# More planned reserve behind transposing DMAs, and loads one group further ahead, in a fused attention and MLP kernel

## Chip, cores, metric

The kernel runs on one core of a Trainium2 chip. The metric is the device time of one execution in microseconds (us). An engine is named as in the profile: PE is TensorE, PEld its weight loads, DVE VectorE, ACT ScalarE, POOL GpSimd, SP SyncE. SP computes nothing here; it issues transposing DMAs. POOL issues nearly all loads, ACT the stores.

## What is computed

Sliding-window attention over 8 batches of 8 heads, 576 positions of 64 channels, followed by a two-layer MLP on the 4608 resulting rows.

```python
scores = q @ k.T / sqrt(64)                      # per batch and head
scores = where(abs(i - j) <= 32, scores, -1e9)
attn = softmax(scores) @ v
x = attn.transpose(0, 2, 1, 3).reshape(4608, 512)
h = maximum(x @ w_in, 0.0)                       # w_in: 512 x 2048
out = (h * h) @ w_out                            # w_out: 2048 x 512
```

Inputs and output are float32; the kernel works in bf16 with float32 sums.

## The kernel before, in words

**Tiles.** Attention is cut into 24 groups G = 3b + g, of 192 query rows each (three per batch b). A group's two windows of keys give its scores by 16 small matmuls (L547); ACT takes the exponential (L571), DVE multiplies with the band mask (L576), PE multiplies with v (L604), DVE normalises into `xa` and `xb` (L626). The MLP works on tokens: the first layer (`mm1`, L719) in blocks of 192, 256 or, from token 2048 on, 512 tokens, each cut into pieces of up to 16 matmuls that share one PSUM bank; ACT takes the relu (L725), DVE squares it into `gt` (L728). The second layer (`mm2`, L739) works on blocks u of 128 tokens, each in four segments of four 128x512 matmuls. "Block 13.0" is segment 0 of u = 13.

**How data come to their places.** For each group POOL issues two loads of k and two of q (L376, `load_qk`) and two of v (L425, `load_v`); they cast to bf16. q and k must be transposed before the scores. For the first two batches (groups 0 to 5) PE does this (`turn_pe`). From group 6 on SP does it by transposing DMAs (L506, `turn_dma`), two for k and two for q. The attention result is transposed as well, into `xt`: by PE for groups 0 to 2, by two SP DMAs from group 3 on, one from `xa` (64 rows, L699) and one from `xb` (128 rows, L702). A first-layer block needs the `xt` of all its tokens.

**Who sets the order.** The program records every operation with an engine, what it reads and writes, a planned duration and a key, and then plans the whole run with a list scheduler (`schedule`): whenever an engine is free in the plan, it takes the ready operation with the lowest key. The result is a fixed order on each engine. On the chip each engine works through its list and waits on semaphores where an input isn't there yet; planned times themselves are not enforced. So a constant of the plan changes nothing but the order.

**Keys.** One unit is 64 tokens. A group's scores have key 3G - 13 (`LEAD`), its SP transposes 3G - 16, its `xt` transposes 3G - 12.8 and 3G - 12.5; a piece of the first layer has its token number / 64 (plus a share for its place in the block), a segment of the second layer 2u + 9 + seg / 2.

**What the plan assumes of a DMA.** It is issued for `dur` ns (for a transposing DMA `TISS` = 1340), queued, served as so many packets of so many ns (`move`), and its data count as landed after a further `LANDQ` (2000 ns) plus a `slack` of its own:

```python
dma=(f"t{t}{G % 6}", G), key=key, dur=TISS, move=(h // 4, TMOVE), name=f"td{t}{b}{g}", slack=TSLACK)   # L508
it[3].end = now + LANDQ + it[3].slack                                                                  # L163
```

`TSLACK` belongs to the q and k transposes (h // 4 is 20 to 28 packets), `XSLACK` to the two `xt` transposes (16 and 32 packets), and `TMOVE`, ns per packet, to both. Loads have `LSLACK` (5000).

**What releases a load.** A load's key sets its place in the recording, and it also gets a real dependency: `after=self.moe`, the last scores or first-layer piece recorded before it (L378, L428). With the key 3G - 13 - 9 (`AHEAD`) of a group from 6 on, this is the scores of group G - 3. On the chip POOL, which takes its list in order, waits there on a semaphore of PE. Raw q and k have six buffers, as does v, so a group's load may overwrite what group G - 6 has used.

Of the kernel before, what the change touches and what calls it, by code (L numbers as in the profile page):

```python
# [22 lines left out]
LEAD = 13.0  # L23
LAG = 9.0
AHEAD = 9.0
TISS = 1340
TMOVE = 25
NVR = 24
VKEY = 10.0
TSLACK = 1000  # L30
XSLACK = 1000
LSLACK = 5000
NCLR = 1
LANDQ = 2000
# [232 lines left out]
class Gen:  # L267
# [233 lines left out]
    def turn_dma(self, t, b, g, key):  # L501
# [3 lines left out]
        for x in range(2):  # L505
            self.p.rec("SP", lambda e, x=x: e.dma_start(dst[:, :, h * x:h * x + h], raw[0:h, x, :], transpose=True),  # L506
                       reads=[("raw", t, G % NRAW, x)], writes=[(t + "t", b % 2, g) if x else (t + "h", b % 2, g)],
                       dma=(f"t{t}{G % 6}", G), key=key, dur=TISS, move=(h // 4, TMOVE), name=f"td{t}{b}{g}", slack=TSLACK)  # L508

# [124 lines left out]
    def xturn(self, G):  # L634
# [4 lines left out]
        if G < NXT:  # L639
# [48 lines left out]
            if two:  # L688
                for x, (c0, c1) in enumerate(((0, 64), (64, 192))):
# [9 lines left out]
        self.p.rec("SP", lambda e: e.dma_start(self.XT[:, :, r:r + 64], xa[64:128, :], transpose=True),  # L699
                   reads=[("xa", G % 3)], writes=wr[:1], dma=(f"xa{G % 3}", G), key=key - 0.3, dur=TISS, move=(16, TMOVE), name=f"T{G}a",  # L700
                   slack=XSLACK)
        self.p.rec("SP", lambda e: e.dma_start(self.XT[:, :, r + 64:r + 192], xb[:], transpose=True),  # L702
                   reads=[("xb", G % 3)], writes=wr[1:], dma=(f"xb{G % 3}", G), key=key, dur=TISS, move=(32, TMOVE), name=f"T{G}b", slack=XSLACK)

# [76 lines left out]
    def build(self):  # L781
        p = self.p
        self.k1 = 0
        self.moe = None
        K = -100.0
        self.setup_idle()
        self.setup_iota(K + IOTA)
        self.setup_id(K)
        self.setup_mask(2, K + 1)
        self.setup_bias(2, K + 1.1)  # L790
        self.setup_mask(1, K + 2)
        self.setup_bias(1, K + 2.1)
        self.setup_k(0, K + 0.5)
        self.setup_v(0, K + 1.5)
        self.setup_v(1, VSET[0])
        self.setup_v(2, VSET[1])
        self.setup_mask(0, MKEY[0])
        self.setup_mask(3, MKEY[1])
        for i in range(3, NV):
            self.setup_v(i, -9)  # L800
        self.setup_k(1, -9)
        for n, it in enumerate(self.opening()):
            kd, a = it[0], it[1:]
            key = K + n
            if kd == "w1":
                self.load_w1(a[0], key)
            elif kd == "w2":
                self.load_w2(a[0], key)
            elif kd == "v":
                self.load_v(*divmod(a[0], 3), key, a[1:])  # L810
            elif kd[0] == "h":
                self.load_hw(kd[1], a[0], key)
            else:
                self.load_pair(kd, *divmod(a[0], 3), key)
        for g in (1, 2, 4, 5):
            self.copy_v(g, K + 7 if g < 3 else 3 * g - LEAD - AHEAD)
        todo = []

        def at(key, f, *a):
            todo.append((key, len(todo), f, a))  # L820

        for G in range(NG):
            b, g = divmod(G, 3)
            if b > 1:
                key = 3 * G - LEAD - AHEAD
                for t in "kq":
                    at(key, self.load_pair if G < NPAIR else self.load_qk, t, b, g, key)
                at(key, self.load_v, b, g, key)
                if g and G < NVR:
                    key = 3 * G - LEAD - 0.5 if G >= VCS else key  # L830
                    at(key + 0.01, self.copy_v, G, key - VKEY if G >= VCS else key)
            for t in "kq":
                key = 3 * G - LEAD - (0.6 if b < NTURN else 3)
                at(key, self.turn_pe if b < NTURN else self.turn_dma, t, b, g, key)
            for ws in ((0,), (1,)) if G < NSPLIT else ((0, 1),):
                at(3 * G - LEAD + 0.3 * ws[0], self.scores, G, ws)
            for w in range(2):
                at(3 * G - LEAD + 0.3 * w + 0.1, self.pv, G, w)
            at(3 * G - LEAD + 0.5, self.xturn, G)
        t0 = 0  # L840
        while t0 < NTOK:
            n = FIRST[t0] if t0 in FIRST else 192 if t0 < 768 else 256 if t0 < T512 else 512
            m = min(512 // n, 4)
            for d in range(0, 16, m):
                key = t0 / 64 + d / 16 * n / 64
                at(key, self.mm1, t0, n, list(range(d, d + m)), key)
            t0 += n
        at(500, self.mm2_last, NBLK - 1, 500)
        for u in range(NBLK - 1):
            for seg in range(4):  # L850
                at(2 * u + LAG + seg * 0.5, self.mm2, u, seg, 2 * u + LAG + seg * 0.5)
        for key, _, f, a in sorted(todo, key=lambda x: x[:2]):
            f(*a)
        p.schedule()
        with self.nc.Block():
            dsems, dcount = p.emit()
            for s in dsems:
                if s[0] == "o":
                    self.nc.sync.wait_ge(dsems[s], dcount[s])
# [35 lines left out]
```

## Time and profile before

| | |
|---|---|
| median of 3 runs | 302.69 us (302.65 to 303.72) |
| the profiled execution: own time | 303.58 us |
| its span, first to last instruction | 301.5 us |
| granted PE clock | 1.000 |
| first layer, L719 | 144.6 us in 896 matmuls |
| second layer, L739 | 139.2 us in 560 matmuls |
| SP transposes of q and k, L506 | 72, 1.25 us each to issue (median), landing 2.3 / 5.6 / 8.2 us after issue (least, median, most) |
| POOL waiting for scores before a load | 78.6 us in 15 waits |

Busy times of one engine add up to more than the span, because matmuls overlap in the array: the start-to-start distance of two matmuls says more than the duration of one. A line of the timeline gives start, duration, engine, line, operation, out<-in, the count of instructions merged into it, and in brackets the idle time before it with the releaser that the profile infers. The releaser is the one that came last by the semaphore records; where that engine's result is no input, it was another, often a DMA. In a table by stretches each engine has its busy time and in brackets its instructions; then come the granted clock, the share of the DMA engines (over 1 where packets overlap) and GB/s.

The 16 DMA engines are busy in 27 of the page's 40 slices, up to some 210 us, when the last loads and most transposes are done; after that mostly output is written. POOL has nothing more to do from 198 us on.

### The profile page before, as it was taken

What the parts mean: (1) busy time and instruction counts of PE and PEld (TensorE: products, weight loads), DVE (VectorE), ACT (ScalarE), POOL (GpSimd) and SP (SyncE); (2) the same over time, 40 slices, a digit from 0 to 9 for tenths busy, and PEclk for the clock granted to TensorE, in tenths of its full rate; (3) what the DMA queues carried; (4) which work ended last, traced back from release to release, by engine and by line L of the source; (5) the groups of instructions that cost most, each with busy time, mean ns of one, the idle gap of its engine ahead of it and who ended that gap; (6) DMA issues with size and microseconds to landing.
All of it is one profiled execution on the core that took longest, in us unless ns stands there. A gap on an engine that the chain in (4) does not pass through costs nothing.

```text
span 301.5 us, 6250 instructions
## 1 busy us (share of the span) xinstructions
PE 294.1 (98%) x2431; PEld 171.2 (57%) x2431; DVE 166.7 (55%) x385; ACT 161.5 (54%) x250; POOL 107.2 (36%) x143
## 2 busy tenths in 40 slices
PE   7899999999999999999989999999999999999997
PEld 3488876757667777664444545444445444444445
DVE  6898786736677776655756656456456322222100
ACT  4487845746456676644656645646636344443312
POOL 8992326526546654454664526320000000000000
PEclk9999999999999999999999999999999999999999
DMA  9999999999999999999999999994111200100112
GB/s 171 176 205 184 195 178 164 160 221 154 189 155 187 154 151 160 163 154 195 127 176 185 176 151 138 185 126 105 55 37 55 67 35 35 37 35 36 37 70 104
DMA packets 160636, 39.83 MB, mean 132 GB/s; under 512 B 149984, under 2 KB 156128, under 8 KB 160608
## 3 DMA queue, kind: packets, MB, share of 16 engines
q0 software_dynamic: 106016, 17.93, 82.8%
q1 hardware_dynamic: 49264, 12.14, 29.0%
q10 hardware_dynamic: 5328, 9.37, 9.4%
q8 instruction: 19, 0.31, 0.4%
q14 instruction: 9, 0.07, 0.1%
HBM read 36.70 MB, written 9.44 MB: 153 GB/s over the span
## 4 chain that ended last, share of the span: by engine, by line
PE 90%; DMA 5%; POOL 3%; DVE 1%; ACT 0%; issue 0%; POOLq 0%; ACTq 0%
PE ht L719 40%; PE outp L739 40%; DMA w<-in_moe_w_in_dram 5%; PE at L547 4%; PE at L604 4%; POOL v L425 1%; POOL w L438 1%; PE at L467 1%; PE ht L764 1%; PE outp L764 1%; POOL kpair L408 1%; POOL qpair L408 1%; ACT rt L725 0%; DVE gt L728 0%; DVE xa L626 0%
## 5 line engine op out<-in xcount | busy, mean ns | idle before, releaser
L719 PE MATMUL ht<-xt,w 128*128 128x256 bf16 (+2 forms) x896 | 144.6, 303 | 0.2 <-DMA w<-in_moe_w_in_dram 0.2
L739 PE MATMUL outp<-w,gt 128*128 128x512 bf16 x560 | 139.2, 379 | 0.0
L725 ACT ACTIVATE rt<-ht 128x512 bf16<-128x512 f32 (+1 forms) x152 | 86.3, 577 | 87.8 <-PE ht L719 83.9
L719 PEld LDWEIGHTS ht<-xt,w 128*128 128x128 bf16 x896 | 81.0, 98 | 43.6 <-DMA w<-in_moe_w_in_dram 0.3
L728 DVE TENSOR_TENSOR gt<-rt 128x512 bf16<-128x512 bf16 (+1 forms) x152 | 61.6, 408 | 61.2 <-ACT rt L725 59.2
L739 PEld LDWEIGHTS outp<-w,gt 128*128 128x128 bf16 x560 | 52.3, 98 | 55.3 <-ACT oe L749 0.8
L376 POOL DMA_DIRECT2D kraw<-in_k_dram x36 | 27.8, 780 | 89.9 <-PE at L547 78.6
L571 ACT ACTIVATE e<-at 128x1024 bf16<-128x1024 f32 x46 | 44.8, 1021 | 11.4 <-PE at L547 11.3
L576 DVE TENSOR_TENSOR pt<-e,mask 128x1024 bf16<-128x1024 bf16 x46 | 31.8, 691 | 31.6 <-ACT e L571 31.5
L425 POOL DMA_DIRECT2D v<-in_v_dram x48 | 37.9, 802 | 0.0
L749 ACT ACTIVATE oe<-outp 128x512 f32<-128x512 f32 x35 | 21.0, 599 | 26.8 <-PE outp L739 26.8
L376 POOL DMA_DIRECT2D qraw<-in_q_dram x36 | 27.8, 781 | 0.0
L604 PEld LDWEIGHTS at<-v,pt 128*128 128x128 bf16 x384 | 18.0, 98 | 9.4 <-DVE at L632 1.4
L604 PE MATMUL at<-v,pt 128*128 128x65 bf16 x384 | 20.1, 194 | 0.3 <-ACT pt L568 0.2
L626 DVE TENSOR_TENSOR xb<-at,rs 128x512 bf16<-128x512 f32 x24 | 16.6, 691 | 1.2
L626 DVE TENSOR_TENSOR xa<-at,rs 64x512 bf16<-64x512 f32 x24 | 16.7, 695 | 0.9
L547 PE MATMUL at<-qt,kt 64*128 64x128 bf16 x384 | 15.2, 217 | 1.7 <-DVE gt L728 1.3
L547 PEld LDWEIGHTS at<-qt,kt 64*128 64x128 bf16 x384 | 10.9, 94 | 10.3 <-issue 6.8
L623 DVE RECIPROCAL rs<-at 64x8 f32<-64x8 f32 (+1 forms) x48 | 10.0, 209 | 9.8 <-PE at L604 8.4
L632 DVE MEMSET at<- 64x520 f32 x23 | 11.3, 492 | 3.5 <-DVE xa L626 2.6
L309 PE MATMUL outp<-zz 128*128 128x512 bf16 x25 | 7.8, 439 | 1.2 <-DVE zz L303 1.2
L771 DVE COPY oe<-ht 128x128 f32<-128x128 f32 x1 | 0.3, 291 | 14.7 <-PE ht L764 14.7
(67 smaller groups left out, 80.3 us busy)
## 6 DMA issues: line engine op xcount, KB each, us to landing
out_dram<-oe ACTq DMA_DIRECT2D x35, 256.0 KB, 3.3
qraw<-in_q_dram POOLq DMA_DIRECT2D x36, 96.0 KB, 5.7
w<-in_moe_w_in_dram POOLq DMA_DIRECT2D x4, 512.0 KB, 10.8
v<-in_v_dram POOLq DMA_DIRECT2D x16, 128.0 KB, 7.7
w<-in_moe_w_out_dram POOLq DMA_DIRECT2D x4, 512.0 KB, 18.5
v<-in_v_dram POOLq DMA_DIRECT2D x16, 96.0 KB, 7.4
kraw<-in_k_dram POOLq DMA_DIRECT2D x12, 112.0 KB, 5.0
kraw<-in_k_dram POOLq DMA_DIRECT2D x12, 96.0 KB, 5.0
```

The source lines that it names most:

```text
L376: self.p.rec("POOL", lambda e, j=j: e.dma_start(raw[0:h, j, :].rearrange("p (h d) -> p h d", h=8), s[:, j]), writes=[("raw", t, G % NRAW, ...
L425: self.p.rec("POOL", lambda e, j=j, lo=lo, hi=hi, k0=k0: e.dma_start(vt[lo - k0:hi - k0, j, :, 0:64], self.v[b, :, lo:hi, :].rearrange("h ...
L547: mm = e.matmul(sc[:, 512 * par + 128 * j:512 * par + 128 * j + 128], kt[r:r + 64, j, k0:k0 + 128], q, start=G >= NBIAS, stop=True, skip_g ...
L571: self.p.rec("ACT", lambda e, e_=e_, sc=sc: e.activation(e_[:], sc, ACTF.Exp, scale=0.125), reads=tags[w], writes=[("e", n % 2)], key=key, ...
L576: self.p.rec("DVE", lambda e, pt=pt, ee=ee, mb=mb: e.tensor_tensor(pt[:], ee, mb, ALU.mult), reads=[("e", n % 2), ("mask", mi)], writes=[( ...
L604: mm = e.matmul(avp[:, c:c + 65], pt[:, 4 * (h % 2) + h // 2, :], vt[:, w, h, 0:65], start=(w == 0 and y == 0), stop=True, skip_group_chec ...
L626: self.p.rec("DVE", lambda e: e.tensor_tensor(x[r0:128, :].rearrange("p (x y c) -> p x y c", x=2, y=4), av[:, :, :, 0:64], rb, ALU.mult), ...
L719: mm = e.matmul(ht[:, n * x:n * x + n], self.W1[:, ft, 128 * d:128 * d + 128], self.XT[:, ft, r:r + n], start=(ft == 0), stop=(ft == 3))
L725: self.p.rec("ACT", lambda e: e.activation(rt[:, 0:c], ht[:, 0:c], ACTF.Relu), reads=[f"ht{k % 2}"], writes=[("rt", k % 4)], key=key, dur= ...
L728: self.p.rec("DVE", lambda e: e.tensor_tensor(gt[:, d0:d0 + len(ds), r:r + n], rr, rr, ALU.mult), reads=[("rt", k % 4)], writes=[("gt", s, ...
L739: mm = e.matmul(op[:], gt[:, d, r:r + 128], self.W2[:, d, :], start=(d == 0), stop=(d == 15))
L749: self.p.rec("ACT", lambda e: e.activation(oe, op[:], ACTF.Copy), reads=[f"outp{u % 2}"], writes=[("oe", u % 4)], key=key, dur=act(512), n ...
```

## The change

It changes constants of the plan and the key of the loads. The planned cost of a packet of a transposing DMA goes from 25 to 15 ns; the reserve after its landing from 1000 to 3500 ns for q and k and to 2500 ns for `xt`. From group 13 on (`GFAR`) a load has key 3G - 13 - 12 in place of 3G - 13 - 9, which makes `self.moe` the scores of group G - 4: loads of 12 wait for scores of 9 as before, loads of 13 for those of 9 too, loads of 14 for those of 10, and so on. No operation is added or removed, and no data take another way.

```diff
 AHEAD = 9.0
+FAR, GFAR = 12.0, 13
 TISS = 1340
-TMOVE = 25
+TMOVE = 15
 NVR = 24
 VKEY = 10.0
-TSLACK = 1000
-XSLACK = 1000
+TSLACK = 3500
+XSLACK = 2500
 LSLACK = 5000
...
         for G in range(NG):
             b, g = divmod(G, 3)
             if b > 1:
-                key = 3 * G - LEAD - AHEAD
+                key = 3 * G - LEAD - (FAR if G >= GFAR else AHEAD)
                 for t in "kq":
                     at(key, self.load_pair if G < NPAIR else self.load_qk, t, b, g, key)
                 at(key, self.load_v, b, g, key)
```

## Prediction

> **What bounds the kernel now.** I read the page's first part, then the busy time by stretch, then TensorE in order of time, then SyncE's queue.
>
> ```profile
> span 301.5 us, 6250 instructions
> PE 294.1 (98%) x2431; PEld 171.2 (57%) x2431; DVE 166.7 (55%) x385; ACT 161.5 (54%) x250; POOL 107.2 (36%) x143
> PE 90%; DMA 5%; POOL 3%; DVE 1%; ACT 0%; issue 0%; POOLq 0%; ACTq 0%
> ```
>
> TensorE (PE) carries the chain. A busy matmul is not yet a packed one, so I look at starts: eight 128x512 matmuls in a row last 1.89 us and one of them 0.379, so they start (1.89 - 0.379) / 7 = 0.216 us apart. Nearly all starts keep that pace. What PE loses after its opening stands in three stretches (columns: stretch, its length, PE busy):
>
> ```profile
> 34.00:150.00 116.00, 115.91 (x1136) 78.02 (x1133) 76.88 (x168) 68.32 (x105) 60.45 (x78) 1.00 1.83 168
> 150.00:153.00 3.00, 1.67 (x22) 0.82 (x21) 1.23 (x3) 1.19 (x2) 0.00 (x0) 1.00 2.41 147
> 153.00:296.00 143.00, 143.00 (x866) 67.42 (x865) 60.42 (x132) 68.85 (x108) 22.91 (x30) 1.00 0.68 90
> ```
>
> The reader is to see that 262 us of the span hold one hole. In order of time it is this:
>
> ```profile
> 149.18 1.89 PE L719 MATMUL ht<-xt,w 128*128 128x512 bf16 x8
> 149.69 0.69 DVE L626 TENSOR_TENSOR xb<-at,rs 128x512 bf16<-128x512 f32 x1
> 151.79 0.42 DVE L728 TENSOR_TENSOR gt<-rt 128x512 bf16<-128x512 bf16 x1 [0.44 <-ACT rt L725]
> 152.40 0.62 PE L547 MATMUL at<-qt,kt 64*128 64x128 bf16 x16 [1.33 <-DVE gt L728]
> ```
>
> The next matmul was due at 149.18 + 8 x 0.216 = 150.91 and starts at 152.40: **1.49 us lost**. It is the scores of group 16 (counting L547: 16 matmuls a group). The named releaser, gt, is no input of scores; the VectorE step they do need, xb, is done at 150.38. What is left is the group's transposed q, the second half of which SyncE (SP) issues at 144.81:
>
> ```profile
> 143.54 1.22 SPq L702 DMA_TRANSPOSE xt<-xb  x1
> 144.81 1.26 SPq L506 DMA_TRANSPOSE qt<-qraw  x1
> 146.16 3.58 SPq L506 DMA_TRANSPOSE kt<-kraw  x2
> ```
>
> The DMA issues of a window around it give that one transfer's time from issue to landing, the last column:
>
> ```profile
> qt<-qraw SPq DMA_TRANSPOSE x1, 7.5
> ```
>
> So it landed at 144.8 + 7.5 = 152.3. A transpose came 1.5 us after the place that the order had given its consumer. The same subtraction for the other groups gives a margin of 2.0 to 5.1 us for groups 6 to 14, 1.0 for 15, 4.0 for 17 and over 4.8 from 18 on.
>
> **Where the order comes from.** Scores of group G have key 3G - 13, the first matmul layer its token number / 64. From group 18 on (169 us) the scores stand on their key; before, they run behind it. There one number repeats: scores of G start 25.5 to 26.5 us after those of G - 3 (98.9 to 125.0, 107.0 to 133.1, 116.0 to 142.1). That is the planned loop: scores of G - 3 release the loads of G, these the transposes, these the scores. Its period per group is 26 / 3 = 8.7 us, and SP issues back to back through it.
>
> **The change part by part.**
>
> *Reserves (TSLACK, XSLACK, TMOVE).* They cost no instruction. A q or k transpose is planned later by 2500 ns less 24 packets x 10 ns = 2260 ns; an xt transpose by 1500 - 160 = 1340 (xa) or 1500 - 320 = 1180 (xb). Scores and first-layer matmuls that were placed by a landing are placed later by that; PE gets second-layer blocks in between. For group 16 alone 2.26 covers the 1.49 us, leaving 0.8.
>
> But the loop of G - 3 to G lengthens too, for groups before 13. Bounds of one turn: 0 (where a queue, not a landing, placed the scores) and 2.26 + 0.86 us (one block of four matmuls, 4 x 0.216, of rounding); I take 2.26, since the constant 26 us says that landings place them. Then groups 6 to 8 come 2.3 us later, 9 to 11 4.5, and 12 6.8 (116.0 to 122.8).
>
> *Loads a group earlier from 13 on.* The same 72 + 36 DMAs; no bytes added. Loads of 13 now wait for scores of 9 (90.5 + 4.5 = 95.0), as those of 12 do, so POOL issues twelve in a row: six took 91.82 to 96.61, so 13's begin at 95.0 + 1.3 + 4.8 = 101.1, against 100.2 now. Behind the wait on POOL stand only later loads. From then on each load runs some 9 us ahead of its present place in the order, and the loop no longer binds. SP does: 2 k, 2 q and 2 xt issues a group, planned 6 x 1.34 = 8.04 us. From 122.8 scores come at about 130.9, 138.9, 147, 155, 163 and 171; group 19, by key at 181, is on time. So the delay (5.9, 5.8, 4.9, 4.1, 1.7, 1.6 us for 13 to 18) is paid back by 181.
>
> *The twelve loads in a row.* The trace has no such pair, so bounds: beside one group's loads q and k transposes land 5.3 and 5.7 us after issue (medians), 8.2 at worst, and 2.4 once loads are gone; beside the opening's long load queue (loads landing 12 to 13 us after issue) xt transposes took 6.5 and 7.2. Lower bound: nothing added, as beside that queue. Upper: the excess over 2.4 doubles, 5.5 to 8.6 at the median and 8.2 to 14.0 at worst. I take nothing, by the opening's row, the only one with more loads queued. The Trainium skill speaks against this edit: DMAs issued by SP, ScalarE and GpSimd run on the same 16 engines and interleave, whichever issued them (DMA: Bandwidth & Descriptors, Issuing engines are not separate DMA queues). By that rule the sum would be that of the burst, a rival below; the 5.5 against 2.4 agrees with it, the opening's 6.5 to 7.2 says that it does not grow with the queue.
>
> *What covers the delay.* PE must have other work while first-layer blocks wait for xt.
> - Tokens from 1024 need xt of group 6. They start at 81.13 with five second-layer blocks left (6.3 and 7.0 to 7.3): dry at 81.1 + 5 x 0.864 = 85.4. Its xt landed at 78.9; with 2.3 more, 81.2. Covered by 4.2 us.
> - Tokens from 2048 need the first xt transpose of group 13. They start at 138.04 with token blocks 13, 14 and 15 left, 12 x 0.864 = 10.4 us: dry at 148.4. It landed at 137.8, 12.8 us after its scores; from 130.9 that is 143.7. Covered by 4.7 us.
>
> If the cover is gone, each us of lateness is a us of span. Opening and end stay: the first transposing DMA is issued at 38.6 us, and from group 19 on the scores stand where they stand now.
>
> *Sum.* 301.5 - 1.5 + 0 = 300.0 us of span. The profiled execution took 303.58, 2.08 outside its span, so 302.1 by its own account. It stands 0.89 above the median of the runs shown (302.69; 302.65 to 303.72). Either the recording adds that, and the median has the whole hole: 302.69 - 1.5 = 301.2; or the median executions have only 0.6 us of it: 302.1. Nothing in the trace separates these, and I take the middle, **301.6**.
>
> **Rivals.**
> - *Late again (0.23).* From group 12 on scores are planned every 8.04 us, but SP's records give 59 issues in 86.9 us from 50.7 to 137.7, 1.47 each, 8.8 a group: 0.76 lost per group, 3.0 over groups 13 to 16. The margin at 12, 2.9 + 2.3 = 5.2, falls to 2.2 at 16, and one slow landing (7.5 against 4.7 for group 15, 2.8) makes it -0.6. Against: during groups 6 to 12 the loop gives SP 28.3 / 3 = 9.4 us a group, so it starts without arrears. A hole of 0.5 to 1.5 us stays: 302.1 to 303.2, say 302.7.
> - *The burst (0.05).* Transposes issued at 95 to 106 us, beside the loads of 12 and 13, land later. Now the last of a group lands 3.8 to 5.6 us after issue there and leaves 2.9 to 5.1 us, plus 2.3. At the median's doubling (8.6 - 3.8 = 4.8 against 5.2) no hole; from 9.0 us on each us is a hole; at the worst's doubling 14.0 - 9.0 = 5.0. Half of that, 2.5, on the profiled execution's 302.1: 304.6.
> - *Reserve runs out (0.12), slower.* At tokens from 2048: if a turn of the loop costs not 2.26 but over 3.9 us, scores of 12 come 11.6 us later, those of 13 after 135.6, and xt lands after 148.4, when second-layer work is gone. From there each us of group 13's lateness costs one. At 4.7 a turn, group 13 comes at 138 and the hole is 2.4: 302.1 + 2.4 = 304.5. For it: landings of up to 8.2 us and a second turn through a queue already back to back. Against: three turns must each cost 1.6 us more than the edit adds.
> - *The loads' edit does nothing by itself* is part of the first case: the k of group 16 had landed by 132.0, its first transpose went out at 137.7, and no wait of SP names a load. Its worth lies in the planned order alone.
>
> **How the numbers follow.** The hole closes and none opens: 0.60, 301.2 to 302.1, down to 300.9 if a 0.25 us gap at 96.4 goes too. A measurement here tells about 0.5% (1.5 us) from no change: faster means under 301.18, which is the lower part of that case, 0.25. Same: the rest of it, 0.35, late again, 0.23, and the burst's smaller half, 0.03: 0.61. Slower: the other 0.02 and the reserve's 0.12: 0.14. The range goes from 300.9 to 303.6 (late again at its worst, 303.2, and 0.4 for holes that burst or reserve leave small), leaving out some 0.05 below and 0.14 above.
>
> **What would show it.** The stretch around 150 us fully busy; scores of 12 near 122.8 and of 19 near 181; loads of 13 straight behind those of 12; first-layer blocks from 2048 near 145 with no hole before; margins of groups 12 to 17 above 0.5 us. Wrong if PE has holes at 140 to 165 us, if the period to group 12 stays 26 us, or if the time moves outside 1.5 us of hole.

## The result and the profile after

| | before | after |
|---|---|---|
| median, lowest to highest, six runs of each on one chip | 303.07 us (302.64 to 307.56) | 305.45 us (304.47 to 308.97) |
| ratio, 95% interval | | 1.0105 (1.0065 to 1.0144) |
| profiled execution, own time | 303.58 us | 305.39 us |
| its span | 301.5 us | 303.4 us |

The kernel became 1.0% slower. The ratio leaves out the run of 307.56 us, a slow one (over 1.5% above the fastest of its kernel), so it isn't the ratio of the two medians. The forecast was 301.6 us, the range ended at 303.6. Lines of the code are one higher in the profile after (the scores are L548, the layers L720 and L740). The first part of its page and its chain of waits:

```profile
span 303.4 us, 6216 instructions
PE 291.1 (96%) x2394; PEld 171.1 (56%) x2431; DVE 165.9 (55%) x385; ACT 160.5 (53%) x250; POOL 107.5 (35%) x143
PE 89%; DMA 5%; POOL 3%; issue 2%; DVE 0%; ACT 0%; POOLq 0%; DVEq 0%
```

37 of 2431 matmul records are missing, so a sum of PE's busy time proves little here; the weight loads (PEld) are all there, and holes are read from starts. What is new in the chain is "issue 2%": PE stood for nothing that a semaphore record names. The table by stretch (stretch, length, PE, PEld, DVE, ACT, POOL busy, then clock, DMA share, GB/s) says where:

```profile
34.00:106.00 72.00, 71.42 (x722) 50.35 (x731) 47.26 (x104) 42.27 (x67) 39.03 (x51) 1.00 1.84 167
106.00:109.00 3.00, 2.21 (x23) 1.50 (x22) 0.70 (x3) 0.32 (x1) 2.56 (x4) 1.00 1.79 144
109.00:143.00 34.00, 33.63 (x313) 22.28 (x316) 21.80 (x46) 19.00 (x29) 18.01 (x24) 1.00 1.80 160
143.00:147.00 4.00, 1.65 (x16) 0.95 (x15) 0.90 (x2) 0.60 (x1) 0.68 (x1) 1.00 1.52 195
147.00:296.00 149.00, 147.74 (x913) 70.35 (x930) 67.36 (x149) 74.96 (x118) 22.93 (x30) 1.00 0.78 94
```

The hole at 151 is gone, as foretold: scores of group 16 start 5.0 us after their last transpose. Two others are there instead, and they lie ahead of first-layer blocks. TensorE in order of time, around both:

```profile
104.93 1.89 PE L740 MATMUL outp<-w,gt 128*128 128x512 bf16 x8
107.61 1.03 PE L720 MATMUL ht<-xt,w 128*128 128x256 bf16 x8 [0.79 <-issue]
...
143.54 0.42 PE L605 MATMUL at<-v,pt 128*128 128x65 bf16 x8
146.31 1.67 PE L720 MATMUL ht<-xt,w 128*128 128x512 bf16 x7 [2.35 <-issue]
147.91 0.62 PE L548 MATMUL at<-qt,kt 64*128 64x128 bf16 x16
```

The block of token 1536 was due at 104.93 + 8 x 0.216 = 106.66 and starts at 107.61: 0.95 us. The block of token 2048 was due 0.26 after 143.54 (that is the distance after such a row elsewhere), at 143.80. Its row has 7 of 8 matmuls (two pieces of four; no piece of the first layer has more than eight), and the scores follow 8 steps after 146.09, so it is the first that is missing and the block began one step earlier, 146.31 - 0.22 = 146.09: 2.3 us. At that moment seven second-layer segments of tokens below 2048 were still to be done; they run after it, up to 168 us. PE had work that it could have done, but its list had the block first. What the block waits for is its first xt transpose, in SyncE's queue and in the DMA issues of a window around it:

```profile
138.64 1.21 SPq L700 DMA_TRANSPOSE xt<-xa  x1
```

```profile
xt<-xa SPq DMA_TRANSPOSE x1, 7.2
```

138.64 + 7.2 = 145.9, and PE goes on within 0.2 us. For token 1536 the same holds: its transpose landed at 107.5.

**What the loads do now.** POOL in order of time, and what it waited for:

```profile
94.71 1.63 POOL L377 DMA_DIRECT2D kraw<-in_k_dram  x2 [6.71 <-PE at L548]
...
99.48 1.56 POOL L377 DMA_DIRECT2D kraw<-in_k_dram  x2
...
104.07 1.50 POOL L377 DMA_DIRECT2D kraw<-in_k_dram  x2
```

Groups 12, 13 and 14 leave in one row of 18 loads: the scores of 10, which those of 14 wait for, start at 101.51, while POOL is still issuing. Later the queue stays as long. Medians from issue to landing, the last column, for what was issued at 110 to 165 us, first before, then after:

```profile
qraw<-in_q_dram POOLq DMA_DIRECT2D x14, 96.0 KB, 5.6
...
kt<-kraw SPq DMA_TRANSPOSE x14, 6.2
qt<-qraw SPq DMA_TRANSPOSE x13, 4.7
xt<-xa SPq DMA_TRANSPOSE x6, 5.6
xt<-xb SPq DMA_TRANSPOSE x6, 4.7
```

```profile
qraw<-in_q_dram POOLq DMA_DIRECT2D x12, 96.0 KB, 13.3
...
kt<-kraw SPq DMA_TRANSPOSE x14, 7.8
qt<-qraw SPq DMA_TRANSPOSE x13, 7.6
xt<-xb SPq DMA_TRANSPOSE x6, 8.1
xt<-xa SPq DMA_TRANSPOSE x6, 7.2
```

A load takes more than twice as long, a transpose 1.6 to 3.4 us longer, and that for 50 us, not for one burst.

### The profile page after: what moved, and what is told of

Read it like the earlier page. It is cut to its first block, busy times and chain, and to the rows that moved or that the text cites. A ratio compares the mean times of both kernels' runs of the same rounds, so it can differ in the third digit from the quotient of the medians.

```text
span 303.4 us, 6216 instructions
## 1 busy us (share of the span) xinstructions
PE 291.1 (96%) x2394; PEld 171.1 (56%) x2431; DVE 165.9 (55%) x385; ACT 160.5 (53%) x250; POOL 107.5 (35%) x143
## 4 chain that ended last, share of the span: by engine, by line
PE 89%; DMA 5%; POOL 3%; issue 2%; DVE 0%; ACT 0%; POOLq 0%; DVEq 0%
PE ht L720 40%; PE outp L740 40%; DMA w<-in_moe_w_in_dram 5%; PE at L605 4%; PE at L548 4%; POOL v L426 1%; POOL w L439 1%; PE at L468 1%; PE ht L765 1%; PE outp L765 1%; POOL qpair L409 1%; POOL kpair L409 1%; DVE xb L627 0%; ACT oe L750 0%; ACT oe L775 0%
## 5 line engine op out<-in xcount | busy, mean ns | idle before, releaser
L720 PE MATMUL ht<-xt,w 128*128 128x256 bf16 (+2 forms) x887 | 142.3, 302 | 4.5 <-issue 3.3
L740 PE MATMUL outp<-w,gt 128*128 128x512 bf16 x534 | 134.0, 379 | 1.6 <-issue 0.3
L720 PEld LDWEIGHTS ht<-xt,w 128*128 128x128 bf16 x896 | 80.9, 98 | 46.9 <-issue 3.7
L740 PEld LDWEIGHTS outp<-w,gt 128*128 128x128 bf16 x560 | 52.2, 98 | 55.9 <-ACT oe L750 1.1
L548 PE MATMUL at<-qt,kt 64*128 64x128 bf16 x384 | 15.2, 217 | 0.3 <-DVE mask L334 0.2
L548 PEld LDWEIGHTS at<-qt,kt 64*128 64x128 bf16 x384 | 10.8, 94 | 8.3 <-issue 7.0
L310 PE MATMUL outp<-zz 128*128 128x512 bf16 x23 | 7.1, 444 | 1.2 <-DVE zz L304 1.2
```

The source lines that it names most:

```text
L548: mm = e.matmul(sc[:, 512 * par + 128 * j:512 * par + 128 * j + 128], kt[r:r + 64, j, k0:k0 + 128], q, start=G >= NBIAS, stop=True, skip_g ...
L720: mm = e.matmul(ht[:, n * x:n * x + n], self.W1[:, ft, 128 * d:128 * d + 128], self.XT[:, ft, r:r + n], start=(ft == 0), stop=(ft == 3))
L740: mm = e.matmul(op[:], gt[:, d, r:r + 128], self.W2[:, d, :], start=(d == 0), stop=(d == 15))
```

## The experiments

Ratios are to the kernel before, run on the same chip. Two theories stood at the start. **Traffic**: loads a group earlier keep the DMA queues full, transposes land later, and that alone costs the time. **Order**: the longer reserves shift the order, and that costs it.

### Each half alone

The reserves and the packet cost without the earlier loads:

```diff
-                key = 3 * G - LEAD - (FAR if G >= GFAR else AHEAD)
+                key = 3 * G - LEAD - AHEAD
```

> The change without its second half: the new reserves, all loads waiting three groups back. Two theories. TRAFFIC: the loads that run a group earlier keep the DMA rings full, transposes land 7 to 8.7 us after issue where they took 4.5 to 5.6, and the xt of group 13 comes late for that. ORDER: the longer reserve lengthens the chain from scores to scores, so that the xt of group 13 comes late with any traffic. TRAFFIC: transposes land in 5 to 6 us again, the hole ahead of token 2048 is under 1 us, 302 to 303.5. ORDER: scores of 13 stay at 129 us or later, the hole stays at 2 us or more, 304.5 to 306.

Measured: 302.58 us, 0.9991 (0.9968 to 1.0013). Transposes land 5.0 to 6.4 us after issue, token 2048 starts at 141.79, 0.2 us after its transpose, with no hole.

The earlier loads without reserves and packet cost (against the kernel before):

```diff
+FAR, GFAR = 12.0, 13
-                key = 3 * G - LEAD - AHEAD
+                key = 3 * G - LEAD - (FAR if G >= GFAR else AHEAD)
```

> The change's second half alone: loads from group 13 on wait four groups back, reserves as before. TRAFFIC: transposes land in 7 to 8.7 us from 95 us on, with the smaller reserve of before, so holes at least as large as with the whole change: 305 to 308. ORDER: the chain keeps its 26 us for three groups, scores of 13 near 125, the hole at group 16 as before or gone: 301.5 to 303.5.

Measured: 302.84 us, 1.0001 (0.998 to 1.0021). Landings are as slow as after the change (7.5 to 8.1 us), and yet nothing is lost: token 2048 starts at 143.03, 0.7 us after its transpose. Neither half costs anything measurable. Both theories in their plain form are wrong: slow landings need not cost anything, if the order leaves room for them.

### The order and the wait taken apart

The next two keep every engine's list as it is planned and change only, once the plan is made, which scores a load of group 13 and later waits for. First the order of before with the wait of after:

```diff
+        for G, gate, o in self.LD:
+            if G >= 13:
+                o.deps.discard(gate)
+                o.deps.add(self.SC[G - 4])
```

(`LD` holds each load `o` with its group and the scores `gate` that it waits for, here those of G - 3. The lines that collect both are left out, and so are those that put the recording, with each engine's list unchanged, into an order that fits the new waits.)

> Every engine's order is that of the kernel before; only the semaphore value changes on which a load of group 13 or later waits (scores four groups back, not three). TRAFFIC: transposes from 95 us on land some 2.5 us later than before; before had margins of 0.2 us ahead of token 2048, 1.0 at scores 15 and -1.5 at 16, so holes of 2 to 4 us more: 305 to 307. ORDER: no loss, 302.5 to 303.5.

Measured: 303.50 us, 1.0036 (1.0007 to 1.0064). Landings of 7.2 to 8.2 us eat the margins (0.04 us at scores 12 and 13, 0.2 at token 2048), with only small holes. The sign was that of the traffic theory, the size (some 0.9 us) far under its 305 to 307.

Then the order of after with the wait of before:

```diff
+        for G, gate, o in self.LD:
+            if G >= 13:
+                o.deps.discard(gate)
+                o.deps.add(self.SC[G - 3])
```

> Every engine's order is that of the changed kernel; only the semaphore value changes on which a load of group 13 or later waits (scores three groups back, not four). TRAFFIC: transposes land in 5 to 6 us, the holes near 107 and 144 us close, 301.5 to 303; against it stands that a transpose on SP may then wait for its load, at most 2 us a group. ORDER: the hole ahead of token 2048 stays at 2 us or more, 305 to 307.

Measured: 302.65 us, 0.9998 (0.9971 to 1.0025), span 300.4 us. Both holes close. By stretch, around the two places:

```profile
106.00:109.00 3.00, 3.00 (x31) 2.23 (x30) 1.66 (x5) 0.60 (x1) 1.58 (x3) 1.00 2.00 181
...
142.00:146.00 4.00, 3.79 (x39) 2.02 (x38) 1.65 (x4) 2.15 (x4) 0.34 (x1) 1.00 1.92 214
```

And the same two rows of TensorE, with the transpose that they need:

```profile
142.71 0.42 PE L625 MATMUL at<-v,pt 128*128 128x65 bf16 x8
143.34 1.67 PE L740 MATMUL ht<-xt,w 128*128 128x512 bf16 x7 [0.21 <-issue]
```

```profile
xt<-xa SPq DMA_TRANSPOSE x1, 5.0
```

(L740 is the first layer here, as the edit adds lines.) With the same list on every engine, token 2048 comes 2.97 us earlier, which is also the difference at the last scores (225.94 against 228.91) and, within 0.1, that of the spans: 303.4 - 300.4 = 3.0. It has two parts: PE reaches the place 143.54 - 142.71 = 0.83 earlier since the hole at token 1536 is gone, and the other 2.14 are the transpose's landing, 5.0 us in place of 7.2. So **the wait and the order cost the time together**: the order of after leaves token 2048 no room for a landing of 7 us. (How far a single landing may be trusted follows below.)

### A burst or a standing queue

Is it the 18 loads in a row, or that one more group is in flight from then on? The change itself ran again beside two variants of it. The change again, without any edit:

> The changed kernel once more, as the reference for the three beside it. With the first four runs the loads' traffic stands as the cause, and two forms of it are left. BURST: the loads of groups 12, 13 and 14 leave POOL in a row (95 to 108 us) and what that backs up is not worked off before 145 us. STANDING: from group 13 on there is always one group more of loads in flight, so a transpose always shares the DMA engines, burst or not. Both: 304.5 to 306, one hole of 2 to 3 us ahead of token 2048 and one of about 1 us ahead of token 1536.

Measured: 307.69 us, 1.0149 (1.0086 to 1.0212), four runs from 305.06 to 309.46. Its profile has the hole at token 2048 again, of 2.3 us; the one at 1536 not.

With the order of after, only group 13 waits four back: the burst of 12 and 13 stays, the standing queue goes.

```diff
+            if G >= 14:
+                o.deps.discard(gate)
+                o.deps.add(self.SC[G - 3])
```

> The changed kernel's order on every engine; only the loads of group 13 wait four groups back, those of 14 and later three back again. This has the double step at 95 us and no standing lead. BURST: the xt ahead of token 1536 comes late as before (a hole near 1 us at 107 us) and landings near 138 us are still 7 us: 303.5 to 305.5. STANDING: from 112 us on landings are 5 to 6 us, the hole ahead of token 2048 closes: 302.3 to 303.3.

Measured: 303.76 us, 1.0014 (0.9994 to 1.0035). Landings are back at 5.2 to 6.4 us; no hole at 2048, 1.0 us at 1536.

With the order of after, a ramp: groups 13, 14 and 15 wait for TensorE steps 1/4, 2/4 and 3/4 of a group earlier than three back, and only those from 16 on wait four back. The burst goes, the standing queue stays.

```diff
+            late = {13: 0.75, 14: 0.5, 15: 0.25}.get(G)
+            if late:
+                t = gate.start + late * (self.SC[G - 3].start - gate.start)
+                o.deps.discard(gate)
+                o.deps.add(min((x for x in p.ops if x.eng == "PE" and x.name != "idle"), key=lambda x: abs(x.start - t)))
```

> The changed kernel's order on every engine; the loads of groups 13, 14 and 15 wait for a PE step a quarter, half and three quarters of a group earlier than scores three groups back, those of 16 and later four groups back. This has the standing lead from group 16 on (about 120 us) and no double step. BURST: landings of 5 to 6 us all along, no hole over 0.5 us: 302.3 to 303.3. STANDING: landings of 7 us and more from 125 us on, the hole ahead of token 2048 stays at 1.5 us or more: 304 to 305.5.

Measured: 304.73 us, 1.0081 (1.0047 to 1.0115). Landings take 7.1 to 7.6 us, and the hole at 2048 is 2.0 us, with none at 1536. The standing queue makes the large hole. The small one at 1536 came in two of the three profiles with the burst, and not without it.

One landing proves little: in the three profiles of the kernel before (two follow below), the transpose that token 2048 waits for took 5.6, 5.2 and 8.5 us. With the order of after it took 7.2, 7.3 and 7.5 us in the three profiles with the standing queue, and 5.0 in each of the two without. The medians over all 36 to 38 transposes issued at 110 to 165 us are firmer: 5.2 to 6.1 us in the seven profiles in which loads of 14 and later wait three groups back, 7.4 to 7.9 in eight of the nine with four; the ninth, without xt reserve, has 5.7 behind its long holes.

### More and less reserve for xt

If token 2048 is only placed too early, `XSLACK` alone must move its hole. Everything else is as after the change:

```diff
-XSLACK = 2500
+XSLACK = 5000
```

> The whole change with 5000 ns of reserve behind the xt transposes in place of 2500; loads wait four groups back as in the change. The order then puts about two segments of the second layer more ahead of token 2048. If the hole is a place in the order that came too early while second-layer work was left, it closes or falls under 1 us: 302.3 to 303.5. If the second layer is used up there, as the prediction's rival had it, the hole only moves behind those segments: 304.5 to 306.

Measured: 303.54 us, 1.0021 (1.0008 to 1.0033). Landings stay at 7.5 to 8.0 us. Two segments of block 14 and the scores of 15 now stand ahead of token 2048, which starts at 146.20, 1.5 us after its landing, with no hole. About a fifth of the loss stays (0.21% of 1.05%); a wait of 0.8 us of the product with v for DVE at 71 us is one place of it, the rest I have not found.

```diff
-XSLACK = 2500
+XSLACK = 0
```

> The whole change with no reserve behind the xt transposes (0 ns in place of 2500), so the order puts token 2048 some five segments of the second layer earlier, while the loads' traffic stays: the opposite step to the 5000 ns run. Two questions. PLACE: the hole ahead of token 2048 grows with the step, to 4 us or more, 307 us or more. CLOCK: in executions of the change with a hole of 2 to 2.5 us some record a granted clock of 0.994 and 2 to 4 us more. If the hole is what lowers the clock, a hole of 4 us or more lowers it in nearly all executions, and the profile shows matmuls at half pace behind the hole: 309 us or more. If not, the time rises by the longer hole alone, at clock 1.000.

Measured: 310.40 us, 1.0255 (1.0197 to 1.0314). Ahead of 2048 PE stands for 2.2 us, not the 4 or more that I had expected, since a hole of 2.7 us ahead of token 1792 has already let the transposes catch up. The last section comes back to this run.

The large reserve with the loads of before, as a candidate for the best of both (against the change):

```diff
-XSLACK = 2500
+XSLACK = 5000
...
-                key = 3 * G - LEAD - (FAR if G >= GFAR else AHEAD)
+                key = 3 * G - LEAD - AHEAD
```

> The reserves of the change with 5000 ns behind the xt transposes in place of 2500, and all loads three groups back as before: what the runs so far point to as the best. The two xt consumers that still start as their data land (ahead of tokens 1536 and 2048, margins 0.1 and 0.2 us with 2500 ns) get 1 us and more; as their waits were under 0.5 us together, 302.2 to 302.8, 0 to 0.4 us under the kernel before. If the longer reserve uses up the second layer, 303 or more.

Measured: 303.38 us, 1.0016 (0.9998 to 1.0033). The margin at 2048 is 5.9 us and nobody needs it; it is no gain.

### Was the hole of before there at all?

The kernel before, profiled twice more, since my forecast took a gain from the one hole in its profile:

> The kernel before, unchanged, in another profiled execution, for the size of its hole ahead of scores 16. The prediction took 1.5 us as what the change can gain. TYPICAL: the hole is again 1 to 2 us in each execution. ONE-OFF: the slow landing of that group's q (7.5 us) belongs to the one execution, the margin at scores 16 is now positive or the hole under 0.5 us, with a span near 300.5 us.

> The kernel before once more, a third execution: as for the second. TYPICAL: a hole of 1 to 2 us ahead of scores 16 again. ONE-OFF: margin there positive or a hole under 0.5 us.

Measured: 303.08 and 303.15 us, spans 301.0 and 301.1. The scores of 16 start 1.7 and 4.1 us after their last transpose, with no hole. In the first of them:

```profile
150.14 1.89 PE L719 MATMUL ht<-xt,w 128*128 128x512 bf16 x8
151.96 0.62 PE L547 MATMUL at<-qt,kt 64*128 64x128 bf16 x16
```

The scores follow straight on the first layer. The landing of 7.5 us that made the hole was that of one execution.

### Packet cost or interaction

One question was left: the earlier loads cost nothing alone, but 3 us with the rest of the change. Which part of the rest? Either the planned 15 ns a packet, by which the plan takes a full queue for too fast; or the longer reserves. Two corners with the earlier loads: the change with 25 ns, and the change with the old reserves, both against the change.

```diff
-TMOVE = 15
+TMOVE = 25
```

> The whole change, with the planned cost of a transposing packet back at 25 ns (15 in the change). PACKET: the loss comes from counting a full queue too short; with 25 ns the order has more second-layer work ahead of token 2048 and the hole closes: 302.5 to 303.8, though transposes still land in 7 to 8 us. INTERACTION: the longer reserves with the earlier loads lose by themselves; a hole of 1.5 us or more stays: 304.5 or more.

Measured: 302.50 us, 0.9993 (0.9981 to 1.0005). TensorE where token 2048 starts:

```profile
146.08 0.62 PE L548 MATMUL at<-qt,kt 64*128 64x128 bf16 x16
146.86 0.81 PE L740 MATMUL outp<-w,gt 128*128 128x512 bf16 x3 [0.16 <-issue]
147.50 1.89 PE L720 MATMUL ht<-xt,w 128*128 128x512 bf16 x8
```

The block starts at 147.50, behind the scores of 15 and 4 segments more than after the change (of the last of them the first record is missing); its transpose was issued at 137.9, took 7.0 us and landed at 144.9, 2.6 us ahead. Landings are as slow as ever (7.0 to 8.0 us). Only its place in the order is other: 147.5 against 143.8, **3.7 us later**.

```diff
-TSLACK = 3500
-XSLACK = 2500
+TSLACK = 1000
+XSLACK = 1000
```

> The loads' wait four groups back, and 15 ns a packet, with the reserves of before (1000 ns). PACKET: the loads' wait alone was 302.8; with 15 ns the order puts token 2048 before its data by 3 us or more, and other consumers too: 306 or more, with a granted clock under 1 in some executions. INTERACTION: without the longer reserves 15 ns does little: 302.5 to 303.8.

Measured: 309.24 us, 1.02 (1.0166 to 1.0234). Two places stand open, at token 1536 (1.8 us) and at token 2048, the latter here:

```profile
141.01 3.32 PE L720 MATMUL ht<-xt,w 128*128 128x512 bf16 x8 [3.06 <-DMA xt<-xa]
```

Fifteen segments were still to be done. The corners side by side:

| loads from 13 on | ns a packet | reserves | ratio to before |
|---|---|---|---|
| three back | 15 | 3500 / 2500 | 0.9991 |
| four back | 25 | 1000 / 1000 | 1.0001 |
| four back | 25 | 3500 / 2500 | 0.9993 |
| four back | 15 | 3500 / 2500 (the change) | 1.0105, 1.0149 |
| four back | 15 | 1000 / 1000 | 1.02 |

With loads four back the packet cost decides. With loads three back 15 ns costs nothing beside the long reserves; beside the old ones it was not run. The longer reserves do no harm; they make the harm of the other two smaller.

The plan's own lines say why 10 ns weigh so much. It serves one queue at a time and goes to the next after so many ns:

```python
spent += it[2]                     # ns of one packet
if spent >= ((180 if now < 30000 else PQ) if q == "POOL" else HWB if now < 30000 else 60):
```

With loads waiting, POOL's turn is seven packets of 14.5 ns, 101.5 ns (`PQ` is 100). SP's turn is four packets at 15 ns (60) but three at 25 ns (75). A group has about 4 x 24 + 16 + 32 = 144 transposing packets: 144 / 4 x 161.5 = 5.8 us at 15 ns, 144 / 3 x 176.5 = 8.5 us at 25 ns, worked out from the code. SP is planned to issue them every 6 x 1.34 = 8.04 us. So with 25 ns the plan sees a queue of transposes that grows as long as loads keep theirs full, and puts other work first; with 15 ns it sees one that drains.

The planned times of these kernels, which `schedule` works out from the code, bear this out. From issue to landing, reserve left out, the SP transposes planned at 110 to 150 us have a median of 5.2 us with 15 ns, whether loads wait three groups back or four: such a plan doesn't see the standing queue. With 25 ns it is 6.0 us three back, and four back 9.2 with the old reserves and 8.3 with the long ones. On the chip it was 5.2 to 6.1 and 7.4 to 7.9 us (above). The transpose that token 2048 waits for is planned to take 4.9 us after the change and 8.5 with 25 ns, and the block to start at 142.8 and 147.4 us.

## Why the prediction was wrong, point by point

- **The gain (wrong).** "1.49 us lost" was real in that execution, and the change does remove it, but the two other profiles of before have no such hole. I asked whether "the recording adds that" or the median has it, and took the middle. The median had next to nothing of it: with the order of after and no hole at all, a kernel takes 302.65 (0.9998). I forecast -1.1 us where there was nothing to gain.
- **The twelve loads in a row (the step that failed, together with the next).** "I take nothing, by the opening's row." That row does not say nothing: its xt transposes took 6.5 and 7.2 us, and those of the loop in the same profile 5.7 (`xa`) and 4.6 (`xb`, medians at 90 to 165 us), so like beside like it says 0.8 to 2.6 us more. The doubt was priced as a burst of two groups, with holes at the scores of 12 and 13, at 0.05. There were eighteen loads in the row, not twelve, and the burst was a minor part (0.95 us, at a place that I had not looked at, token 1536). What costs is that one more group of loads is always in flight: I priced the step from one state to the other, and not the state. Transposes took 7.2 to 8.1 us for 50 us, within the bounds that I had written (5.5 to 8.6 at the median), of which I took the lower. The Trainium skill's rule that I set aside (DMA: Bandwidth & Descriptors, Issuing engines are not separate DMA queues) held: with the same lists on every engine, loads of POOL a group earlier made a transpose of SP land after 7.2 us in place of 5.0.
- **The packet cost (mis-sized).** I took off "24 packets x 10 ns" for a transfer by itself, 0.24 us, and 0.16 for the xt one. Beside a full queue it moved the planned landing of that xt transpose by 3.6 us (from 8.5 to 4.9 us after issue) and token 2048 by 3.7. I had read the plan's reserve, and not its server. This step and the one before it need each other: late landings with 25 ns cost nothing (0.9993), nor do 15 ns without late landings (0.9998).
- **The covers (right in size, wrong question).** "Dry at 148.4, covered by 4.7 us": second-layer work was indeed left, seven segments. But PE takes its list in order. A cover helps only if the list has it ahead of the late block, and with the plan taking the transposes for quick, it did not. I had counted the work that was left, and not where it stands. The xt itself came at 145.9 where I had 143.7, although the scores of 13 came 1.4 us earlier than forecast: 16.4 us after them, not 12.8. Of the 3.6 us more, 1.7 are the landing (7.25 us for 5.59), 2.0 a later place in SP's list (issued 9.2 us after the scores, before 7.2).
- **The loop (right in kind, a little large).** Scores of 9 came at 93.37 (forecast 95.0), of 12 at 121.33 (122.8), of 13 at 129.46 (130.9): three turns cost 5.3 us, not 6.8, which is 1.8 a turn. Loads of 13 stood right behind those of 12, from 99.48 (forecast 101.1). Group 19 came at 182.80 (181), later by the holes. The margins of 12 to 17 are all above 0.5 us (0.53 at 13 the least).
- **The rivals.** The reserve that runs out gave 304.5, close to what came, but by a dried-up second layer and a loop of over 3.9 us a turn; neither is there, and the number is luck. The burst gave 304.6 by late scores of 12 and 13; theirs came in time (2.4 and 0.5 us), so that is luck too. Late again did not happen: scores have 3.8 us and more from group 14 on.
- **The sum, mended.** The order of after with loads three back takes 302.65; with the two holes, 0.83 + 2.14 = 2.97: 305.6. The 2.97 are read from the result's own profile, so this adds up and tests nothing. Measured: 305.45 on one chip, 307.69 on another, where three of four runs recorded a lowered clock (below).

No version beats the kernel before by more than the measurement can tell: the change with 25 ns (0.9993) and the reserves alone (0.9991) are level with it.

## What to carry to other kernels

Where a fixed order stands behind a plan, an assumed cost of a transfer is worth what it does to the plan's queue, not its own few ns: ask whether the planned queue drains or grows under the new load. Loads that are issued earlier gain nothing if nobody waited for them, and here they made every transpose slower for as long as the deeper queue stood; change the depth and the assumed transfer times together, or neither. And a single hole in one profile is a gain only if a second profile has it.

## What the hardware showed beside this

**A hole of 2.7 us halved TensorE's clock for 3.4 us.** In the run without xt reserve (`XSLACK` 0), around the hole ahead of token 1792, by stretch (the granted clock is the third number from the end):

```profile
117.50:120.20 2.70, 0.12 (x4) 0.00 (x0) 1.38 (x4) 0.51 (x1) 0.00 (x0) 0.90 1.80 154
120.20:123.10 2.90, 2.76 (x14) 1.99 (x15) 0.22 (x1) 0.60 (x1) 0.00 (x0) 0.50 1.88 156
123.10:126.00 2.90, 2.90 (x33) 1.92 (x32) 0.92 (x3) 2.12 (x4) 0.30 (x1) 1.00 1.85 159
142.00:146.00 4.00, 1.76 (x9) 0.69 (x8) 1.39 (x2) 1.19 (x2) 4.00 (x6) 1.00 1.59 216
```

The rows of TensorE show what that does to sixteen matmuls of one shape, 1.91 us ahead of the hole and 3.23 after it:

```profile
115.46 1.91 PE L720 MATMUL ht<-xt,w 128*128 128x256 bf16 x16
117.21 0.42 PE L605 MATMUL at<-v,pt 128*128 128x65 bf16 x8
120.34 3.23 PE L720 MATMUL ht<-xt,w 128*128 128x256 bf16 x16 [2.72 <-DMA xt<-xb]
```

PE stood for 2.72 us. The clock is 0.50 in the 2.90 us from 120.2 on, and a mean of 0.90 in the 2.70 us before is another 0.54 us at half: some 3.4 us. It fell at about 119.7, 2 us into the hole, so that PE lost half of the 2.75 us from 120.34 to 123.09: 1.4 us. The hole of 2.24 us ahead of token 2048 in the same execution left it at 1.00. In the earlier loads with 15 ns the hole was 3.06 us, and the clock stood at 0.50 from 141.31 to 144.72, all of it behind the hole: 1.7 us lost.

The traces' clock records add something on where it can fall. The stretches at full clock ahead of and behind these two falls are whole multiples of 3.413 us (112.64 is 33 of them, 184.32 is 54; 136.53 is 40, 163.84 is 48), and both stretches at half clock are one such step. In the step that ended in the fall PE stood for 2.05 us in the first case and for 3.06 in the second. The most in a step with no fall behind it was 2.03 us (the change, 144.06 to 147.47), and the hole of 2.24 us lay across a border, 0.53 and 1.71 us. So it seems that what counts is how much of a hole falls into one step, and about 2 us sufficed; two falls do not show the limit.

A mean clock of 0.994 or 0.995 over a whole execution is about one such step (1.7 us lost of some 305). It stands in 2 of 6 runs of the change, 3 of 4 of its repetition and 2 of 7 of the ramp, whose profiled executions kept the full clock with PE standing for 1.9 to 2.1 us, and in 3 of 4 each of the two kernels with 2.7 and 3.1; no other run whose clock is on record has one. Of the ten runs of the change and its repetition, the five at full clock took 304.47 to 305.51 us and the five at 0.994 306.74 to 309.46, medians 3.3 us apart. The step at half clock gives at most 1.7 us of that. None of these five was profiled, so the rest stays open; longer holes would give it, and would also lower the clock.

The Trainium skill (TensorE: Matmul & The Clock Gate, HAM oscillation — how this bites in real kernels) names as its abstract rule no idle gaps of over about 3.4 us. Here 2.72 us sufficed, so the measurement decides: a hole of 2 us or more is priced with a chance of up to 1.7 us on top of its length.

**Landing times vary between executions of one kernel.** The same transpose of before (the last of group 16) landed 7.5 us after issue in one profile, and 5.1 and 4.6 in two others, without any edit.
